# Attention with normalised q and k, then a gated spatial MLP, on one core: the orders of all engines laid out anew, exps that write tokens in natural order, weights and gains loaded otherwise

## The chip, the cores and the metric

One Trainium2 chip, of which the kernel uses one core. A core has a matrix engine (TensorE, PE in the profile; its weight loads are shown apart as PEld), a vector engine (VectorE, DVE), a scalar engine that evaluates functions (ScalarE, ACT), a general engine (GpSimd, POOL) and SyncE (SP), which here issues DMAs only. Operands lie in SBUF, 128 partitions wide; PE writes its results to the eight banks of PSUM, which ACT and DVE read and POOL can't. All engines run at the same time, each through its own queue, in order, and wait for each other by semaphores. The metric is the time of one execution on the device, in microseconds (us).

## What is computed

```python
# q, k, v: (8, 12, 448, 64); all float32
q_n = q / sqrt(mean(q*q, -1) + 1e-6) * g_q
k_n = k / sqrt(mean(k*k, -1) + 1e-6) * g_k
attn = softmax(q_n @ k_n.T / sqrt(64))             # per batch and head, 448 x 448
x = (attn @ v).transpose(0, 2, 1, 3).reshape(8, 448, 768)
h = maximum(x @ w_in, 0)                           # (8, 448, 1024)
u, v = h[..., :512], h[..., 512:]
v_n = (v - mean(v)) / sqrt(var(v) + 1e-6)          # over the 512
v_s = einsum('ts,bsd->btd', w_spatial, v_n) + b_spatial[None, :, None]
out = (u * v_s) @ w_out                            # (8, 448, 768)
```

## The kernel before

The program is a text, `PLAN`: each word names a step, its arguments, the buffers or PSUM banks it takes (after the first slash) and, where there is a choice, the engine (a ACT, v DVE, g POOL, s SP; after the second). The words are carried out from first to last when the program is built, each by the function `op_` of that name, and so the text fixes the order on every engine's queue. There is no scheduler behind it; only the waits are added.

Work is cut into 24 groups of four heads, three to a batch (group G is batch G // 3). A group's q and k come each as a tile of 128 x 2 x 448 numbers: a partition holds seven neighbouring tokens of one head, so that token = 7 p + c, with p the partition's place in its head (64 of them) and c from 0 to 6. The steps of a group:

- `L` (SP) loads raw q (second argument 0) or k (1), 448 KB each. Group 0 comes in four halves of 224 KB, `l.i.r`, and its later steps have small letters for the halves.
- `Q` squares the tile (ACT, POOL or DVE), `R` sums over 64 numbers (DVE), `I` and `J` make 1/rms by a Ln and an Exp (ACT), `N` multiplies and writes bf16 (POOL or DVE).
- `T` turns the tile by a DMA transpose from SBUF to SBUF (SP), and `Z` scales a turned k with the product of the gains (DVE or ACT). In groups 1 to 3 PE turns the tile by seven transposes, `P`, and `K` brings it back from PSUM, scaled if it is a k; for group 0 these are `p` and `k`.
- `S.G.u` makes scores, eight matmuls on parts of the array into two banks, and `E.G.u` takes their exp, 128 x 896 numbers from PSUM to bf16 in SBUF (ACT). There are seven of each per group, 168 in all. The columns of a score bank are q's tokens in the order (c, p).
- `s`, `a`, `b` are passes: they multiply the exps by ones (the softmax's sum) and by the two halves of v. Where the last argument is 1, a step does two groups side by side. `D` and `d` (ACT) make 1/sum, `X` (DVE) scales and writes xt, the turned x.

Then for each batch: `V` and `W` make v's half of x @ w_in, `c` its relu (DVE or ACT), `B`, `M`, `m`, `A` the normalisation, `U` and `u` the other half, `H` the product with the turned w_spatial, `G` the gate, `O` the product with w_out, `o` its copy to SBUF (ACT or DVE), `t` the store. `W.b` also has the last 64 rows of batch b - 1's `O`.

POOL issues the DMAs that cast to bf16: v (`v`), w_in (`wi`), w_spatial (`ws`), w_out (`wo`). `Y` turns w_spatial on PE and `y` copies it to SBUF. Every token axis stays in the order (c, p), so `Y` reads every seventh column of w_sp, the bias is brought into that order by a cast on DVE (`wx`, L337), and `t` writes two DMAs per tile, each of 64 rows that lie seven rows apart in the output. `z.n` issues n dummy matmuls of 128 columns, which compute nothing that is used. `gA`, `gB`, `gC` make a column of g_q * g_k / 8 from two small loads that ACT issues ahead of all else.

DVE and POOL instructions that use both read ports are made to wait for each other, by `port`.

Lines of the profile: L241 and L242 the gains' loads, L260 dummies, L293 and L297 `L` and `l`, L314 `v`, L321 `wi`, L348 `Y`, L361 and L363 copies on ACT and DVE, L367 gA, L380 and L382 squares on ACT and on the others, L393 `R`, L426 `N`, L434 `n`, L445 `P`, L453 `p`, L481 `T`, L506 `S`, L514 `E`, L539 passes, L558 and L562 `D` and `d`, L568 `X`, L575 and L577 relus, L584 `V`, L608 `W`, L645 `U`, L659 `H`, L673 `O`, L690 stores.

Of the kernel before, what the change touches and what calls it, by code (L numbers as in the profile page):

```python
# [25 lines left out]
n.0.1//g p.1.1/0 L.6.1/0 I.2//a S.1.6/67 k.1.1//v S.1.3/12 J.2//a S.1.1/34 L.5.1/1 E.1.6/2/a N.2.0/2/g z.3/f y.0//v  # L26
p.0.1/0 E.1.3/3/a S.1.0/67 k.0.1//v z.10/5 E.1.0/4/a v.0.0//g P.2.0/2 N.2.1/3/v L.6.0/4 z.4/5 E.1.1/5/a wi.1.1//g
s.1.0.0/7 S.1.2/01 Q.3.1/1/v wi.0.2//g P.2.1/6 E.1.2/6/a S.1.4/34 wi.1.0//g z.5/5 K.2.0/2/v E.1.4/7/a Q.4.0/2/g
S.0.3/01 K.2.1/2/v s.1.1.0 s.1.2.0 E.0.3/8/a s.1.3.0 R.3.1//v S.1.5/23 a.1.0.0/6 S.0.6/45 E.1.5/9/a a.1.1.0 Q.4.1/0/g
S.0.5/01 R.4.0//v a.1.2.0 E.0.6/a/a s.1.4.0 s.1.5.0 s.1.6.0 S.2.0/23 E.0.5/b/a b.1.0.0/5 wi.0.0//g Q.3.0/1/v b.1.1.0  # L30
b.1.2.0 b.1.3.0 v.0.3//g E.2.0/c/a S.2.2/01 a.0.0.0/4 a.1.3.0 R.3.0//v Q.5.0/2/g a.1.4.0 D.1/0/a a.1.5.0 a.0.1.0
E.2.2/d/a a.1.6.0 S.0.4/23 R.4.1//v z.4/7 I.3//a S.0.2/01 wi.0.1//g J.3//a E.0.4/e/a b.1.4.0 N.3.0/0/v b.1.5.0
wi.1.2//g b.1.6.0 s.0.0.0/7 E.0.2/f/a s.0.1.0 wi.0.3//g s.0.2.0 N.3.1/1/v S.2.4/23 s.0.3.0 wi.1.3//g z.2/b d.1//a
s.0.4.0 S.2.1/01 I.4//a s.0.5.0 X.1.1//v s.0.6.0 J.4//a z.5/b E.2.1/g/a N.4.1/2/g X.1.0//v P.3.0/5 D.0/1/a P.3.1/6
K.3.0/3/v E.2.4/h/a S.2.3/01 s.2.0.0/7 K.3.1/3/v s.2.1.0 N.4.0/3/g T.4.1/0 b.0.0.0/5 E.2.3/i/a b.0.1.0 R.5.0//v
b.0.2.0 s.2.2.0 b.0.3.0 d.0//a S.3.1/23 b.0.4.0 b.0.5.0 E.3.1/j/a Q.5.1/1/g S.2.5/01 T.4.0/1 b.2.0.0/6 b.2.1.0 b.0.6.0
E.2.5/k/a S.2.6/23 X.0.1//v a.0.2.0 z.2/b L.7.1/5 a.0.3.0 E.2.6/4/a b.2.2.0 Q.6.1/0/g R.5.1//v S.3.3/01 s.2.3.0
s.2.4.0 E.3.3/5/a s.2.5.0 S.3.0/23 a.2.0.0/5 a.2.1.0 I.5//a a.2.2.0 a.2.3.0 R.6.1//v J.5//a s.2.6.0 E.3.0/6/a
N.5.1/0/g a.0.4.0 a.2.4.0 a.0.5.0 a.0.6.0 Q.6.0/2/a b.2.3.0 a.2.5.0 X.0.0//v b.2.4.0 b.2.5.0 D.2/0/a b.2.6.0 R.6.0//v
N.5.0/1/g a.2.6.0 T.5.1/1 S.3.2/01 d.2//a S.3.4/23 U.0.2.0/7 E.3.2/3/a X.2.1//v U.0.2.1 V.0.1.0/4 X.2.0//v v.1.1//g  # L40
# [36 lines left out]
N.13.1/0/g B.2.1//v t.0.3 U.2.2.0/4 E.11.0/2/a V.2.0.2 L.15.0/3 B.2.3//v E.11.2/9/a S.11.6/56 T.13.0/1 S.10.4/23
v.3.4//g U.2.2.1 c.2.0//v E.10.4/4/a U.2.2.2 Z.12/0/v v.3.2//g O.1.0.0/7 T.13.1/1 u.2.2//v E.11.6/k/a N.14.0/3/g
# [82 lines left out]
def kernel(  # L161
# [101 lines left out]
    where = {}  # L263
# [60 lines left out]
    def op_ws(sl, e):  # L324
        pool.dma_start(out=w_sp, in_=moe_w_spatial.rearrange("(p c) s -> p c s", c=C))
# [407 lines left out]
```

## Time and profile before

| | us |
|---|---|
| median of 3 runs (281.03 to 284.57) | 282.72 |
| span of the profiled execution | 277.8 |
| PE busy in it | 261.4 |
| ACT busy | 216.8 |
| DVE busy | 198.7 |
| POOL busy | 155.6 |

The span is the time from the first to the last instruction of one profiled execution; the time of an execution has in addition what lies around that, and the median of the runs is 4.9 us over the span. An instruction group's row gives its line, engine, operation, tiles, shapes and count, then its busy time in us and the mean of one in ns, then the idle time just before its instructions and what ended it. A busy PE is not a PE at its peak: matmuls are pipelined, and the end of one is modelled. The granted clock of TensorE was 0.997 of full speed over the span.

### The profile page before, as it was taken

What the parts mean: (1) busy time and instruction counts of PE and PEld (TensorE: products, weight loads), DVE (VectorE), ACT (ScalarE), POOL (GpSimd) and SP (SyncE); (2) the same over time, 40 slices, a digit from 0 to 9 for tenths busy, and PEclk for the clock granted to TensorE, in tenths of its full rate; (3) what the DMA queues carried; (4) which work ended last, traced back from release to release, by engine and by line L of the source; (5) the groups of instructions that cost most, each with busy time, mean ns of one, the idle gap of its engine ahead of it and who ended that gap; (6) DMA issues with size and microseconds to landing.
All of it is one profiled execution on the core that took longest, in us unless ns stands there. A gap on an engine that the chain in (4) does not pass through costs nothing. (4 is left out here: it accounts for less than half of the span.)

```text
span 277.8 us, 10117 instructions
## 1 busy us (share of the span) xinstructions
PE 261.4 (94%) x4373; PEld 137.4 (49%) x4373; DVE 198.7 (72%) x351; ACT 216.8 (78%) x353; POOL 155.6 (56%) x130
## 2 busy tenths in 40 slices
PE   4799999979999999999999989999998999999993
PEld 4686464435545455354445444453553545455551
DVE  2478978695997997987995677966975174747740
ACT  1399999878999999998999979998898766420632
POOL 3287987987687598957875758645980000000000
PEclk9999999999999999999999999999999999999998
DMA  6989996999989999899999999966589400014586
GB/s 165 331 264 273 176 174 112 217 163 267 257 144 293 311 245 202 179 253 150 257 212 273 228 257 259 181 93 70 75 136 179 161 2 2 18 41 113 138 272 218
DMA packets 62967, 51.14 MB, mean 184 GB/s; under 512 B 39561, under 2 KB 58506, under 8 KB 62922
## 3 DMA queue, kind: packets, MB, share of 16 engines
q1 hardware_dynamic: 54690, 42.22, 64.5%
q0 software_dynamic: 8224, 8.27, 21.2%
q8 instruction: 34, 0.56, 0.8%
q14 instruction: 11, 0.09, 0.1%
q10 hardware_dynamic: 8, 0.00, 0.0%
HBM read 38.55 MB, written 11.01 MB: 178 GB/s over the span
## 5 line engine op out<-in xcount | busy, mean ns | idle before, releaser
L514 ACT ACTIVATE et<-ps 128x896 bf16<-128x896 f32 x168 | 145.7, 921 | 15.0 <-PE ps L506 13.4
L426 POOL TENSOR_TENSOR nrm<-raw,rs 128x896 bf16<-128x896 f32 x43 | 72.2, 1690 | 25.9 <-ACT rs L411 10.1
L506 PE MATMUL ps<-qT,kT 64*32 64x448 bf16 x1344 | 60.2, 354 | 2.5 <-DMA qT<-nrm 1.9
L382 POOL TENSOR_TENSOR sqt<-raw 128x896 f32<-128x896 f32 (+1 forms) x31 | 50.9, 1654 | 17.2 <-DVE vn L636 7.4
L393 DVE TENSOR_REDUCE ss<-sqt 128x14 f32<-128x896 f32 x46 | 48.4, 1075 | 5.0 <-ACT sqt L380 3.8
L539 PE MATMUL ps<-et,vt 64*32 64x448 bf16 x1344 | 48.4, 350 | 2.8 <-DMA vt<-in_v_dram 2.6
L645 PE MATMUL ps<-xt,w_in 128*128 128x448 bf16 x192 | 43.1, 353 | 0.0
L568 DVE TENSOR_TENSOR xt<-ps,rc 128x448 bf16<-128x448 f32 x48 | 28.3, 620 | 14.9 <-ACT rc L562 8.0
L673 PE MATMUL ps<-w_out,gt 128*128 128x384 bf16 x192 | 36.5, 326 | 0.1
L506 PEld LDWEIGHTS <-kT 64*32 64x32 bf16 x1344 | 21.5, 90 | 29.6 <-issue 22.0
L584 PE MATMUL ps<-w_in,xt 128*128 128x512 bf16 x144 | 35.6, 380 | 0.0
L539 PEld LDWEIGHTS <-vt 64*32 64x32 bf16 x1344 | 23.6, 92 | 17.3 <-DMA vt<-in_v_dram 3.9
L664 DVE TENSOR_TENSOR gt<-ps,us 128x448 bf16<-128x448 f32 x32 | 19.3, 620 | 13.0 <-PE ps L659 8.7
L361 ACT ACTIVATE os<-ps 128x384 f32<-128x384 f32 (+1 forms) x33 | 15.9, 493 | 15.4 <-PE ps L673 14.6
L659 PE MATMUL ps<-w_spT,vn 128*128 128x448 bf16 (+1 forms) x128 | 27.7, 353 | 0.0
L645 PEld LDWEIGHTS <-w_in 128*128 128x128 bf16 x192 | 17.0, 98 | 20.5 <-issue 7.3
L539 PE MATMUL ps<-et,ones 64*32 64x448 bf16 x672 | 26.2, 350 | 0.2 <-ACT et L514 0.2
L673 PEld LDWEIGHTS <-gt 128*128 128x128 bf16 x192 | 18.2, 98 | 15.4 <-issue 2.5
L314 POOL DMA_DIRECT2D vt<-in_v_dram x36 | 24.1, 673 | 0.0
L577 DVE TENSOR_SCALAR vs<-ps 128x512 bf16<-128x512 f32 (+1 forms) x24 | 16.3, 684 | 10.4 <-PE ps L584 6.8
L363 DVE COPY os<-ps 128x384 f32<-128x384 f32 (+1 forms) x31 | 16.9, 554 | 8.9 <-PE ps L673 7.7
L620 DVE BATCH_NORM_STATS2 s<-vs 128x6 f32<-128x512 bf16 (+1 forms) x32 | 21.9, 683 | 1.4 <-ACT vs L575 0.9
(62 smaller groups left out, 253.1 us busy)
## 6 DMA issues: line engine op xcount, KB each, us to landing
out_dram<-os SPq DMA_DIRECT2D x56, 192.0 KB, 3.2
raw<-in_q_dram SPq DMA_DIRECT2D x23, 448.0 KB, 5.5
raw<-in_k_dram SPq DMA_DIRECT2D x23, 448.0 KB, 7.0
vt<-in_v_dram POOLq DMA_DIRECT2D x24, 112.0 KB, 5.2
vt<-in_v_dram POOLq DMA_DIRECT2D x12, 224.0 KB, 7.0
w_in<-in_moe_w_in_dram POOLq DMA_DIRECT2D x8, 192.0 KB, 6.1
w_out<-in_moe_w_out_dram POOLq DMA_DIRECT2D x1, 768.0 KB, 11.3
raw<-in_k_dram SPq DMA_DIRECT2D x2, 224.0 KB, 2.6
```

What stands on the lines that cost most here:

```text
L314: pool.dma_start(out=vts[b % 2][64 * halves[0]:64 * halves[0] + 64 * len(halves), g].rearrange("p r c d -> p r (c d)"), in_=src)
L382: port(eng, eng.tensor_tensor(out=t, in0=x, in1=x, op=ALU.mult))
L393: dve.tensor_reduce(out=sss[G % 3][:, i].rearrange("p r c -> p (r c)"), in_=sqt[where.pop(("sq", G, i))].rearrange("p r (c d) -> p (r c) d ...
L426: port(eng, eng.tensor_tensor(out=nrm[sl[0]].rearrange("p c r d -> p r c d"), in0=raw[where["raw", G, i]].rearrange("p r (c d) -> p r c d" ...
L506: pe.matmul(out=ps[at:at + 32, sl[n], 0:S], lhsT=kT[64 * r:64 * r + 64, c, 64 * hh + 32 * x:64 * hh + 32 * x + 32], rhs=qT[64 * r:64 * r + ...
L514: act.activation(out=ets[sl[0]], in_=ps[:, a:b + 1:b - a, 0:S], func=AF.Exp, bias=0.0, scale=1.0)
L539: pe.matmul(out=ps[32 * l:32 * l + 32, where[kind, G][0], 0:S], lhsT=w, rhs=et_of(G, r, c)[at:at + 64], start=(n == 1), stop=(n == C), til ...
L568: dve.tensor_tensor(out=xts[b % 2][:, 2 * g + half, :], in0=ps[:, where.pop(("ab"[half], G))[0], 0:S], in1=rcs[where["rc", G]], op=ALU.mult)
L584: pe.matmul(out=ps[:, bank, :], lhsT=xts[b % 2][:, j, 128 * m:128 * m + 128], rhs=w_in[:, j % 2, j // 2, DH:], start=(n == 1 and j == 2 * ...
L645: pe.matmul(out=ps[:, bank, 0:S], lhsT=w_in[:, j % 2, j // 2, 128 * f:128 * f + 128], rhs=xts[b % 2][:, j, :], start=(n == 1 and j == 2 * ...
L659: pe.matmul(out=ps[:, sl[0], 0:S], lhsT=vns[b % SLOTS["vn"]][rows, m, 128 * f:128 * f + 128], rhs=w_spT[rows, m, :], start=(m == 0), stop= ...
L673: pe.matmul(out=ps[:, sl[0], 0:384], lhsT=gts[b % 2][:, f, 128 * m:128 * m + 128], rhs=w_out[:, f, 384 * h:384 * h + 384], start=(f == 0), ...
```

## The change

All of `PLAN` is rewritten, and some steps with it:

- `E` reads PSUM in the order (p, c), so that exps, and everything behind them, have tokens in their natural order. The inner step of its read is 64 words of four bytes; it writes without gaps, as before.
- w_sp lies as 112 partitions x 4 x 448 and is turned by 16 transposes (49 before), which read it without gaps. The bias is cast by a DMA of POOL straight into w_spT; `wx` is gone.
- `t` stores a tile of 128 rows as one DMA of rows that follow each other, or a half of its columns. There are 34 stores, 56 before.
- w_in comes as six DMAs (eight before), and `V.b.m.g` and `U.b.f.g` need those of their own g alone. The passes g of an accumulation are no longer in the order 0, 1, 2.
- The k gain's load is issued by POOL, ahead of everything else there; g_q stays with ACT.
- 5.1 and 7.0 are turned by PE too (`P` 8 times, 6 before; `T` 38, 40 before).
- Engines, before and after: `Q` ACT 14 and 10, DVE 2 and 6; `N` POOL 43 and 38, DVE 3 and 8; `c` ACT 8 and 17; `K` ACT 1 and 0; the halves' squares `q` DVE 2 and 0, POOL 1 and 3. Between the first and the last exp ACT has 3 `Q` less, 8 `c` and 3 `o` more and a `K` less.
- Dummies: 13 `z` steps with 124 matmuls, then 12 with 183.
- Behind the last `E` there stood 7 `s`, 7 `a`, 7 `b`, 24 `U`, 9 `V`, 21 `O`, 8 `H`, 2 `W`; now 2 `s`, 7 `a`, 2 `b`, 24 `U`, 9 `V`, 22 `O`, 8 `H`, 2 `W`.
- Counted in exps that stand between them, the first step `T` of a group that DMA transposes turn is 4 to 14 ahead of its first `S` before; now 0 to 15, with 3 or less in groups 4, 11, 12, 16, 17 and 21. `N` is 5 or more ahead in both.

The beginning of `PLAN`, and the code:

```diff
-setup//v l.1.0/0 ws//g l.0.0/1 v.0.2//g L.1.0/2 v.0.1//g L.1.1/3 z.30/7 l.0.1 l.1.1 L.2.0/4 L.2.1/5 q.1.0/0/v L.4.1/6
-gA//v gB/7 q.0.0/1/v L.3.1/7 z.33/6 r.0.0//v gC//v r.1.0//v Q.1.0/2/a L.4.0/8 i.0//a R.1.0//v j.0//a n.1.0//g
-Q.1.1/2/a n.0.0//g p.1.0/7 z.7/6 q.0.1//a R.1.1//v q.1.1//g p.0.0/6 k.1.0/0/a Y.1/5 k.0.0/0/v I.1//a Y.3/7 J.1//a
-r.1.1//v y.1//a Y.2/4 N.1.0/0/g Q.2.0/2/a r.0.1//v Y.0/5 y.3//v i.1//a y.2//v Q.2.1/0/a S.0.1/01 R.2.0//v N.1.1/1/g
-S.0.0/23 L.3.0/2 j.1//a P.1.0/7 E.0.1/0/a R.2.1//v z.12/6 K.1.0/1/a n.1.1//g P.1.1/1 L.5.0/3 z.7/6 E.0.0/1/a K.1.1/1/v
...
+setup//v l.0.0/0/s gA//v q.0.0/0/g l.1.0/1/s q.1.0/1/g l.0.1//s q.0.1//g r.1.0//v L.1.0/2/s z.60/f z.2/f gB/0 r.0.0//v
+gC//v r.0.1//v Q.1.0/2/a L.1.1/3/s ws//g l.1.1//s i.0//a L.2.0/4/s v.0.3//g R.1.0//v j.0//a n.1.0//g L.2.1/5/s
+L.3.0/6/s Q.1.1/0/a z.50/f p.1.0/1 q.1.1//a n.0.0//g R.1.1//v I.1//a v.0.0//g v.0.1//g k.1.0/0/v L.3.1/7/s J.1//a
+N.1.0/0/v z.7/f p.0.0/2 k.0.0/0/a z.22/f P.1.0/3 Q.2.0/2/a S.0.2/45 L.4.1/8/s N.1.1/1/g v.0.2//g S.0.0/67 r.1.1//v
+S.0.1/01 i.1//a j.1//a L.5.1/2/s E.0.2/0/a E.0.1/1/a E.0.0/2/a K.1.0/1/v n.0.1//v z.10/f P.1.1/2 z.4/f p.0.1/4
+Q.2.1/0/g K.1.1/1/v z.4/f S.1.1/05 k.0.1//v S.1.3/16 R.2.0//v n.1.1//g R.2.1//v Y.1/7 E.1.1/3/a E.1.3/4/a S.1.2/23
...
-    act.dma_start(out=g_row[:, 1], in_=bass.AP(tensor=g_k.tensor, offset=g_k.offset, ap=[[0, 1], [0, 2], [1, D]]))
+    pool.dma_start(out=g_row[:, 1], in_=bass.AP(tensor=g_k.tensor, offset=g_k.offset, ap=[[0, 1], [0, 2], [1, D]]))
...
-    def op_wi(sl, e, half, l):
-        x = bass.AP(tensor=moe_w_in.tensor, offset=moe_w_in.offset + (64 * l + 32 * half) * DF,
-                    ap=[[DF, 32], [256 * DF, NG], [1, DF]])
-        pool.dma_start(out=w_in[32 * l:32 * l + 32, half, :, :], in_=x)
+    def op_wi(sl, e, g, half):
+        x = bass.AP(tensor=moe_w_in.tensor, offset=moe_w_in.offset + (256 * g + 32 * half) * DF,
+                    ap=[[64 * DF, 4], [DF, 32], [1, DF]])
+        pool.dma_start(out=w_in[:, half, g, :], in_=x)
...
-        pool.dma_start(out=w_sp, in_=moe_w_spatial.rearrange("(p c) s -> p c s", c=C))
+        pool.dma_start(out=w_sp, in_=moe_w_spatial.rearrange("(c p) s -> p c s", p=RW))
...
-        sync.dma_start(out=oss[-1][64:65, 0:S], in_=moe_b_spatial.rearrange("(o s) -> o s", o=1))
+        pool.dma_start(out=w_spT[64:65, 3, :], in_=moe_b_spatial.rearrange("(o s) -> o s", o=1))
...
-        for a in range(n):
-            for c in range(C):
-                pe.matmul(out=p_[64 * a:64 * a + 64, T * c:T * c + T],
-                          lhsT=w_sp[:, c, :].rearrange("q (p c) -> q c p", c=C)[:, 2 * m + a, :],
-                          rhs=ident[0:64, 0:64], is_transpose=True, start=(c == 0), stop=(c == C - 1),
-                          tile_position=(0, 64 * a))
+        for c in range(S // RW):
+            pe.matmul(out=p_[0:n, RW * c:RW * c + RW], lhsT=w_sp[:, c, 128 * m:128 * m + n], rhs=ident[0:RW, 0:RW],
+                      is_transpose=True, start=(c == 0), stop=(c == S // RW - 1))
...
-        act.activation(out=ets[sl[0]], in_=ps[:, a:b + 1:b - a, 0:S], func=AF.Exp, bias=0.0, scale=1.0)
+        act.activation(out=ets[sl[0]].rearrange("q n (p c) -> q n p c", c=C),
+                       in_=ps[:, a:b + 1:b - a, 0:S].rearrange("q n (c p) -> q n p c", c=C),
+                       func=AF.Exp, bias=0.0, scale=1.0)
...
-        for par in ((0, 1) if m < 3 else (1,)):
-            engines[(e or "ss")[par]].dma_start(out=out_c[b][2 * m + par if m < 3 else 6], in_=t[64 * par:64 * par + 64])
+        rows = slice(0, 128) if m < 3 else slice(64, 128)
+        cols = slice(0, DM) if h is None else slice(384 * h, 384 * h + 384)
+        assert all(where["o", b, m, n] for n in ((0, 1) if h is None else (h,)))
+        engines[e or "s"].dma_start(out=out[b, 128 * m:128 * m + rows.stop - rows.start, cols], in_=t[rows, cols])
```

More of the change, by code (lines that the diff above doesn't have):

```diff
@@ L26 @@
[L26 to L40, printed above, removed]
@@ L182 @@
     TAIL = 384
+    RW = 112
     scale = 1.0 / math.sqrt(D)
@@ L223 @@
     w_out = const.tile([128, 4, DM], BF, name="w_out")
-    w_sp = const.tile([64, C, S], BF, name="w_sp")
+    w_sp = const.tile([RW, S // RW, S], BF, name="w_sp")
     w_spT = const.tile([128, 4, S], BF, name="w_spT")
@@ L316, in op_v @@
         where.setdefault(("v", b, g), set()).update(halves)
[L318 to L322 removed]
+    def op_wi(sl, e, g, half):
+        x = bass.AP(tensor=moe_w_in.tensor, offset=moe_w_in.offset + (256 * g + 32 * half) * DF,
+                    ap=[[64 * DF, 4], [DF, 32], [1, DF]])
+        pool.dma_start(out=w_in[:, half, g, :], in_=x)
+        where["wi", g, half] = True
     def op_ws(sl, e):
[L325 removed]
+        pool.dma_start(out=w_sp, in_=moe_w_spatial.rearrange("(c p) s -> p c s", p=RW))
     def op_wo(sl, e):
@@ L582, in op_V @@
         for j in (2 * g, 2 * g + 1):
-            assert where["x", b, j] and all(where["wi", h, l] for h in range(2) for l in range(4))
+            assert where["x", b, j] and where["wi", g, 0] and where["wi", g, 1]
             pe.matmul(out=ps[:, bank, :], lhsT=xts[b % 2][:, j, 128 * m:128 * m + 128], rhs=w_in[:, j % 2, j // 2, DH:],
@@ L643, in op_U @@
         for j in (2 * g, 2 * g + 1):
-            assert where["x", b, j] and all(where["wi", h, l] for h in range(2) for l in range(4))
+            assert where["x", b, j] and where["wi", g, 0] and where["wi", g, 1]
             pe.matmul(out=ps[:, bank, 0:S], lhsT=w_in[:, j % 2, j // 2, 128 * f:128 * f + 128], rhs=xts[b % 2][:, j, :],
@@ L654, in op_H @@
         where["H", b, f] = sl[0]
-        assert where["wx"]
+        assert where["wb"]
         for m in range(4):
@@ L682, in op_o, with op_t @@
         where["o", b, m, h] = True
-    out_c = [out[b].rearrange("(p c) m -> c p m", c=C) for b in range(B)]
-    def op_t(sl, e, b, m):
+    def op_t(sl, e, b, m, h=None):
         t = oss[where["os", b, m]]
-        assert where["o", b, m, 0] and where["o", b, m, 1]
-        for par in ((0, 1) if m < 3 else (1,)):
-            engines[(e or "ss")[par]].dma_start(out=out_c[b][2 * m + par if m < 3 else 6], in_=t[64 * par:64 * par + 64])
+        rows = slice(0, 128) if m < 3 else slice(64, 128)
+        cols = slice(0, DM) if h is None else slice(384 * h, 384 * h + 384)
+        assert all(where["o", b, m, n] for n in ((0, 1) if h is None else (h,)))
+        engines[e or "s"].dma_start(out=out[b, 128 * m:128 * m + rows.stop - rows.start, cols], in_=t[rows, cols])
     def op_z(sl, e, n):
```

257 lines of the change are left out of this document (134 added, 123 removed).

## The prediction

> **What bounds the kernel now.** I read the page's first lines, then busy time by stage (columns: busy us of PE, PEld, DVE, ACT, POOL; granted clock; DMA share; GB/s).
>
> ```profile
> span 277.8 us, 10117 instructions
> L514 ACT ACTIVATE et<-ps 128x896 bf16<-128x896 f32 x168 | 145.7, 921 | 15.0 <-PE ps L506 13.4 <-PE ps L539 0.8
> ```
> ```profile
> 0.00:18.56 18.56, 13.09 (x151) 11.94 (x151) 9.21 (x22) 8.02 (x14) 8.18 (x14) 1.00 0.88 258
> 18.56:60.00 41.44, 39.45 (x737) 21.25 (x729) 33.27 (x46) 39.16 (x59) 35.87 (x33) 1.00 1.01 189
> 60.00:233.37 173.37, 169.03 (x3145) 82.91 (x3146) 132.68 (x238) 155.44 (x248) 111.60 (x85) 1.00 0.94 190
> 233.37:272.90 39.53, 39.53 (x364) 21.29 (x348) 23.49 (x48) 13.52 (x31) 0.00 (x0) 1.00 0.42 118
> 272.90:277.80 4.90, 0.29 (x2) 0.00 (x0) 0.00 (x0) 0.65 (x2) 0.00 (x0) 0.80 0.58 189
> ```
>
> Four stages. A ramp of 18.56 us in which no exp runs. A middle of 214.8 us from the first exp to the end of the last, where ACT is busy 39.16 + 155.44 = 194.6 us and PE 208.5. There ACT sets the pace at first (39.16 of 41.44); later both are nearly full, and ACT's waits, 13.4 us in all, are for score matmuls. A tail of 39.5 us with PE busy to the last tenth. Then 4.9 us for the last copies and stores. So a gain must come from an earlier first exp, from fewer waits in the middle, or from less PE work left for the tail.
>
> **The ramp.** The timeline of the ramp (start, duration, instruction, what the idle before it waited for):
>
> ```profile
> 1.69 3.38 PE L260 MATMUL ps<-ident 128*128 128x128 bf16 x30 [1.69 <-POOL ident masks.py:199]
> ...
> 1.97 0.58 ACTq L242 DMA_DIRECT2D g_row<-in_g_k_dram  x1
> ...
> 8.18 0.28 DVE L367 SCALAR_TENSOR_TENSOR g_row<-g_row 1x128 f32<-1x128 f32 x1 [4.18 <-DMA g_row<-in_g_k_dram]
> ...
> 9.02 3.70 PE L260 MATMUL ps<-ident 128*128 128x128 bf16 x33
> ...
> 10.60 0.95 ACT L380 ACTIVATE sqt<-raw 128x896 f32<-128x896 f32 x1 [6.73 <-DMA raw<-in_q_dram]
> ...
> 11.78 0.21 ACT L419 ACTIVATE rs<-ls 128x14 f32<-128x14 f32 x1
> ...
> 12.07 1.84 POOL L434 TENSOR_TENSOR nrm<-raw,rs 128x448 bf16<-128x448 f32 x2 [8.46 <-ACT rs L419]
> ...
> 14.58 3.42 PE L348 MATMUL ps<-ident,w_sp 64*64 64x64 bf16 x49
> ...
> 17.94 0.94 PE L506 MATMUL ps<-qT,kT 64*32 64x448 bf16 x16
> ...
> 18.56 0.92 ACT L514 ACTIVATE et<-ps 128x896 bf16<-128x896 f32 x1 [0.17 <-PE ps L506]
> ...
> 19.21 0.83 PE L260 MATMUL ps<-ident 128*128 128x128 bf16 x12
> ...
> 19.41 0.92 ACT L361 ACTIVATE qT<-ps 128x896 bf16<-128x896 bf16 x1
> ...
> 21.73 1.73 ACT L514 ACTIVATE et<-ps 128x896 bf16<-128x896 f32 x2
> ```
> ```profile
> raw<-in_q_dram SPq DMA_DIRECT2D x1, 224.0 KB, 2.7
> raw<-in_q_dram SPq DMA_DIRECT2D x1, 448.0 KB, 8.9
> ```
> ```profile
> 0.00:5.00 5.00, 3.31 (x30) 3.12 (x30) 1.84 (x9) 1.28 (x1) 2.57 (x9) 1.00 0.58 154
> 5.00:10.00 5.00, 1.56 (x13) 1.48 (x13) 1.79 (x5) 0.00 (x0) 0.00 (x0) 1.00 1.04 245
> ```
>
> Before, three things hold the first exp back. DVE stands on gA for 4.18 us, for a gain row that lands 6.2 us after its issue. ACT's first square waits to 10.60 for a 448 KB load (8.9 us), with w_sp and v loads beside it. And 49 transposes of w_sp, 3.42 us, stand on PE ahead of the first score.
>
> The change takes each away. The k gains are POOL's first DMA; three of the four first half squares move to POOL, ahead of its w_sp and v loads, so no square stands behind gA on DVE any more (the two reductions still do, and gC, which waits for gB behind 62 dummies on PE, holds the reductions of group 1 to about 8, when they aren't due yet); the 16 transposes left of w_sp go behind the first scores, where dummies fill PE anyway, so they cost nothing there (as long as exps set the pace). Worked along: half loads land at 3.4 to 3.9 (2.7 us after issue); POOL's squares, at
>
> ```profile
> L426 POOL TENSOR_TENSOR nrm<-raw,rs 128x896 bf16<-128x896 f32 x43 | 72.2, 1690 | 25.9 <-ACT rs L411 10.1 <-DVE us L577 5.0 <-issue 4.9
> ...
> L393 DVE TENSOR_REDUCE ss<-sqt 128x14 f32<-128x896 f32 x46 | 48.4, 1075 | 5.0 <-ACT sqt L380 3.8 <-POOL sqt L382 0.9
> ...
> L426 DVE TENSOR_TENSOR nrm<-raw,rs 128x896 bf16<-128x896 f32 x3 | 3.2, 1090 | 0.4 <-ACT rs L411 0.4
> ...
> L382 POOL TENSOR_TENSOR sqt<-raw 128x448 f32<-128x448 f32 x1 | 0.9, 931 | 0.0
> ```
>
> 0.93 each, end near 6.2, and only then come w_sp and v.0.3. If the k gains still take 6.2 us they land near 7, and the reductions of half 0 (half of 1075 ns each) end near 8.2, no later than Q.1.0 below. By 5 us 770 KB have come at 154 GB/s, then 245 KB a us: the three half loads and L.1.0 (1120 KB) are in by about 7, L.1.1 (1568 KB) by about 9.3 with w_sp beside it. Q.1.0 0.95, Ln and Exp 0.5 give rs of the first half near 8.9; before it was 11.99. From there two halves on POOL (1.84), transpose and eviction need 3.7: k.0.0 is done near 12.6. But S.0.2 stands behind P.1.0 on PE, and that behind N.1.0 on DVE: L.1.1 9.3, square to 10.3, reduction 11.3, Ln and Exp 11.9, N.1.0 13.0, transposes 13.5; S.0.2 takes 0.6 to its exp, as before (17.94 to 18.56). First exp near 14.0: **-4.5 us**. Lower bound -5.5 (L.1.1 a us earlier). Upper bound 0: the 112 dummies ahead of p.1.0 at 0.112 each (3.38/30, 3.70/33) end near 15, and the first exp comes near 18.5. I take a first third at that pace and the rest at 0.07 (0.83/12, the row that began right behind other work): done by 11, in time.
>
> The Trainium skill, TensorE: Matmul & The Clock Gate, Part 1, says the array runs at half clock until some 3.4 us of sustained work; the granted clock reads 1.00 throughout and cannot show it, but the three dummy rows agree, and by it the dummies end in time.
>
> Then before, ACT copied a qT (0.92) and waited between its first exps: four took from 18.56 to 23.46. The changed order puts three behind each other and that copy on DVE; **-1.0** (bounds -1.5 and 0, if K.1.1 is late).
>
> **The middle.** ACT also gives three squares away (-3 x 0.945) and takes eight relus and three output copies:
>
> ```profile
> L380 ACT ACTIVATE sqt<-raw 128x896 f32<-128x896 f32 x14 | 13.2, 945 | 7.6 <-DMA raw<-in_q_dram 6.7 <-DVE ss L393 0.7
> L361 ACT ACTIVATE os<-ps 128x384 f32<-128x384 f32 x27 | 13.2, 496 | 14.9 <-PE ps L673 14.6
> ...
> L575 ACT ACTIVATE vs<-ps 128x512 bf16<-128x512 f32 x6 | 3.5, 597 | 0.9 <-PE ps L584 0.9
> ...
> L445 PE MATMUL ps<-ident,nrm 128*128 128x128 bf16 x42 | 3.3, 219 | 0.0
> ```
>
> 8 x 0.60 + 3 x 0.50 - 2.8 = +3.5 us, of which the 13.4 us of waits swallow over half: **+1.5** (0 to 3.5). DVE, 33.27 of 41.44 early and 132.68 of 173.37 later, has room for five more norms and four more squares. Two more tiles turned by PE cost 2 x 0.55 (3.3 us for six) and save two DMA transposes: nothing on balance. Each norm or square moved from POOL to DVE saves POOL 1.69 and costs DVE 1.09 on the port that the two take in turns, and POOL has idle time to give: 0. w_in in six loads by group: its consumers come after group 0's exps, so 0, unless the loads on POOL delay N.2 or N.3, +1 at most. The bias goes straight into w_spT, and a cast leaves DVE: 0, DVE had room. The stores, half as many and the same bytes, stand on SP between the same loads: 0.
>
> The chain that ended last has one wait late in the middle, and then PE without a gap:
>
> ```profile
> 205.95 1.79 SPq L481
> 207.85 7.97 DMA qT<-nrm
> 215.95 0.38 PE ps L506 x8
> ...
> 232.99 3.53 PE ps L539 x144
> ...
> 237.78 0.65 PE ps L673 x4
> ```
> ```profile
> ACT et L514 <- PE ps L506: 13.4, 30, 2.0
> ```
>
> Three norms in a row on POOL sent the last transposes late, and the scores and exps behind them waited; the exp at 216.4 is ACT's longest wait for a score in the row of all such waits (13.4 us in 30 times, the longest 2.0). In the changed order N.22 and N.23 stand 10 to 17 exps ahead of their scores (8 to 10 before) and one is on DVE: **-1.5** (0 to -2.0); next late would be T.23.0, four exps ahead.
>
> **The tail** keeps the same work but for passes: 11 double passes are left behind the last exp instead of 21, at 3.53/18 = 0.196 each, -2.0; one more O, +0.65: **-1.3**. What leaves the tail enters a middle where PE is nearly full: **+0.7** (half; 0 to 1.3). The stores' end: 0.
>
> Sum: -4.5 - 1.0 + 1.5 - 1.5 - 1.3 + 0.7 = -6.1, a span of 271.7. The median of the runs, 282.7, is 4.9 over the profiled span; with that, **276.6 us**.
>
> **The rivals.**
>
> (1) The exps slow down. They now read PSUM with 256 bytes from element to element. No row has such a read. Bounds:
>
> ```profile
> L382 DVE TENSOR_TENSOR sqt<-raw 128x448 f32<-128x448 f32 x2 | 1.2, 615 | 1.1 <-DMA raw<-in_k_dram 1.1
> ...
> L337 DVE CAST w_spT<-os 1x448 bf16<-1x448 f32 x1 | 1.0, 968 | 0.0
> ```
>
> The cast read every seventh word: 968 ns where a plain pass over 448 took 615, 1.57 times. At that, an exp takes 1450 ns and 168 of them add 89 us: 366 us. Below nothing isn't possible: the elements are as many. I take 0, by the nearest rows, ACT reading PSUM: 896 elements cost it 0.92 us at 2 bytes an element (the qT copy at 19.41) and 0.921 at 4 (the exps), so its pace there goes by the element and not by the bytes or lines that it touches; the cast was DVE on SBUF. The rival wins from 6.1/168 = 36 ns an exp; from 70 ns the kernel is over 2% slower.
>
> The Trainium skill speaks for this rival: PSUM — Partial Sum Buffer, Specifications, gives PSUM lines of 8 bytes and says a non-contiguous pattern slows matmuls much. That is said of PE's access; no run here shows ACT's, and by it alone the time would lie near this rival's.
>
> (2) PE sets the pace from about 40 us on, the early exps only wait longer later, or the dummies end late: 281 to 283.
>
> (3) Transposes come late: some groups' DMA transposes now stand 3 exps or less ahead of their scores instead of 4 and more. Three waits such as the 2.0 us one and slower recovery would cost the ramp's gain and more: 285 to 290. Against it: SP issues them as soon as the norm is there, and norms stand 5 exps ahead at least in both.
>
> (4) The middle's other waits fall too: 10 of the 13.4 us go, 268 to 271.
>
> **How the numbers follow.** 2% of 282.7 is 5.7 us, about what a measurement of this kernel can tell from no change; faster means under 277.1. The forecast has 0.62 and by its bounds 271 to 283: 0.40 under 277.1, 0.22 within. Rival 1 has 0.20 (0.04 within 2%, 0.16 slower), since nothing in the trace excludes it; rival 2 0.08 (within 0.07, slower 0.01); rival 3 0.06 (0.01, 0.05); rival 4 0.04. Faster 0.44, same 0.34, slower 0.22. The range of 269 to 290 leaves out rival 1 where it costs over 80 ns an exp and half of rival 4.
>
> **What would show it.** First exp near 14 and gA before 5; the exps' mean at 921; no wait of PE for a DMA transpose over 1 us; PE without a gap behind the last exp for about 38 us. An exp mean over 957, or a first exp after 17, would make it wrong.

## The result, and the profile after

| | before | after |
|---|---|---|
| median of the runs, us | 283.64 (281.03 to 285.06, 4 runs) | 375.47 (371.61 to 378.30, 4 runs) |
| ratio of the times, with its 95% interval | | 1.318 (1.303 to 1.333) |
| time of the profiled execution, us | | 377.19 |
| its span, us | 277.8 | 375.4 |
| ACT busy in it, us | 216.8 | 223.0 |
| PE busy in it, us | 261.4 | 288.2 |

The changed kernel is slower by almost a third. The prediction, 276.6 us with a range of 269 to 290, was wrong. The ratio is taken from the two faster of the changed kernel's four executions (spans of 369.8 and 372.0 us), while the profiled one is of the two slower ones, so a difference taken from its span of 375.4 may be 3 to 6 us too large.

Busy time by stage of the changed kernel, cut as before at the first exp, at 60 us, and at the end of the last exp (columns as in the prediction):

```profile
0.00:14.45 14.45, 9.44 (x180) 8.45 (x184) 8.44 (x19) 6.85 (x12) 9.90 (x17) 1.00 0.89 270
14.45:60.00 45.55, 32.68 (x507) 16.01 (x500) 19.63 (x27) 23.13 (x33) 20.81 (x18) 0.63 0.55 116
60.00:333.22 273.22, 208.31 (x3477) 94.07 (x3483) 153.70 (x264) 180.06 (x283) 118.57 (x93) 0.96 0.61 132
333.22:375.40 42.18, 37.76 (x266) 20.52 (x252) 22.29 (x45) 13.02 (x29) 0.00 (x0) 1.00 0.36 132
```

The ramp is 4.1 us shorter (14.45 for 18.56), the end behind the last exp 2.2 us shorter (42.18 for 44.4). The middle has grown from 214.8 to 318.8 us. No engine is full there any more: from 14.45 to 60 ACT is busy for 23.13 of 45.55 us and PE for 32.68, and the granted clock falls to 0.63.

The costliest groups (busy us and mean ns of one, then the idle time just before and what ended it):

```profile
L509 ACT ACTIVATE et<-ps 128x896 bf16<-128x896 f32 x168 | 149.4, 916 | 105.0 <-PE ps L501 32.7 <-PE ps L536 32.3 <-PE ps L581 8.6
L501 PE MATMUL ps<-qT,kT 64*32 64x448 bf16 x1344 | 71.1, 379 | 27.0 <-ACT et L509 26.1 <-DVE vs L574 0.2
L536 PE MATMUL ps<-et,vt 64*32 64x448 bf16 x1344 | 57.0, 376 | 15.5 <-ACT et L509 15.4
L642 PE MATMUL ps<-xt,w_in 128*128 128x448 bf16 x192 | 45.6, 357 | 10.9 <-ACT et L509 10.8
L565 DVE TENSOR_TENSOR xt<-ps,rc 128x448 bf16<-128x448 f32 x48 | 28.2, 620 | 46.6 <-ACT rc L559 17.6 <-ACT et L509 15.9 <-PE ps L536 9.2
```

An exp with its new read takes 916 ns, no more than before (921). What has grown is the idle time ahead of it, from 15.0 to 105.0 us, and much of it ended with work that has nothing to do with scores: 32.3 us with passes (L536), 8.6 with `V` (L581). It goes both ways. `U` (L642) waited 10.8 us for exps, though it reads xt and w_in and writes a bank of its own; `X` on DVE (L565) waited 15.9 us for exps. Before, the exps waited 0.8 us for passes, and neither `U` (L645 there) nor `X` (L568) for an exp:

```profile
L645 PE MATMUL ps<-xt,w_in 128*128 128x448 bf16 x192 | 43.1, 353 | 0.0
L568 DVE TENSOR_TENSOR xt<-ps,rc 128x448 bf16<-128x448 f32 x48 | 28.3, 620 | 14.9 <-ACT rc L562 8.0 <-PE ps L539 6.9
```

One place shows what they are. The timeline of the changed kernel near 62 us (start, duration, instruction, idle time before it):

```profile
61.06 0.39 PE L501 MATMUL ps<-qT,kT 64*32 64x448 bf16 x8
61.20 1.16 DVE L565 TENSOR_TENSOR xt<-ps,rc 128x448 bf16<-128x448 f32 x2 [1.01 <-PE ps L536]
...
62.23 0.92 ACT L509 ACTIVATE et<-ps 128x896 bf16<-128x896 f32 x1 [0.58 <-DVE xt L565]
...
63.19 0.62 DVE L565 TENSOR_TENSOR xt<-ps,rc 128x448 bf16<-128x448 f32 x1 [0.83 <-ACT et L509]
63.20 1.30 PE L642 MATMUL ps<-xt,w_in 128*128 128x448 bf16 x6 [1.76 <-ACT et L509]
...
64.86 0.57 PE L501 MATMUL ps<-qT,kT 64*32 64x448 bf16 x16
65.31 2.54 ACT L509 ACTIVATE et<-ps 128x896 bf16<-128x896 f32 x3 [1.32 <-PE ps L501]
```

By `PLAN`, the exp at 62.23 is `E.3.3`, whose scores lie in banks 2 and 6. They are there by 61.45. Yet the exp waits for an `X` on DVE, which reads group 1's result in bank 4 (`X.1.0`, the first of the two at 61.20; it ends at 61.84); and once it runs, `U.0.2.0`, which writes bank 3, stands on PE until it is over, and `X.2.1`, which reads bank 5, stands on DVE. The next scores, `S.3.1`, stand behind `U` in PE's queue and start at 64.86, so the next exp is late as well. (They take bank 2, which this exp does read, so before its end at 63.15 they could not have started in any case.) Banks 3, 4 and 5 are neither read nor written by this exp. They lie between the two that it reads.

That is the part of the change that neither the list of it nor the prediction names. In the old `PLAN` the two banks of an `S` are always neighbours. In the new one they are in 43 of 168; the others lie 2 to 7 apart (`S.3.3/26`), with 1.9 banks between on average over all. Theory N: the program is put in order, when it is built, as if an exp used everything from its first bank to its last. Two other theories are tried beside it: R, that the new read with its steps of 256 bytes holds PSUM up for PE and DVE, and O, that the new orders of the engines are too tight by themselves.

### The profile page after: what moved, and what is told of

Read it like the earlier page. It is cut to its first block, busy times and chain, and to the rows that moved or that the text cites. A ratio compares the mean times of both kernels' runs of the same rounds, so it can differ in the third digit from the quotient of the medians.

```text
span 375.4 us, 10169 instructions
## 1 busy us (share of the span) xinstructions
PE 288.2 (77%) x4398; PEld 139.1 (37%) x4413; DVE 204.1 (54%) x353; ACT 223.0 (59%) x355; POOL 149.3 (40%) x126
## 4 chain that ended last, share of the span: by engine, by line
PE 58%; ACT 29%; DVE 5%; issue 4%; DMA 2%; SPq 0%; another core or an unknown queue 0%; ACTq 0%; DVEq 0%
ACT et L509 26%; PE ps L536 14%; PE ps L501 10%; PE ps L670 9%; PE ps L642 8%; PE ps L581 6%; PE ps L656 5%; PE ps L605 3%; DMA raw<-in_k_dram 2%; DVE xt L565 1%; DVE ss L388 1%; PE ps L440 1%; ACT rc L555 1%; DVE gt L661 1%; PE ps L264 1%
## 5 line engine op out<-in xcount | busy, mean ns | idle before, releaser
L509 ACT ACTIVATE et<-ps 128x896 bf16<-128x896 f32 x168 | 149.4, 916 | 105.0 <-PE ps L501 32.7
L421 POOL TENSOR_TENSOR nrm<-raw,rs 128x896 bf16<-128x896 f32 x38 | 63.9, 1687 | 75.8 <-ACT rs L406 27.6
L501 PE MATMUL ps<-qT,kT 64*32 64x448 bf16 x1344 | 71.1, 379 | 27.0 <-ACT et L509 26.1
L377 POOL TENSOR_TENSOR sqt<-raw 128x896 f32<-128x896 f32 (+1 forms) x33 | 53.0, 1610 | 59.1 <-DVE vn L633 17.5
L536 PE MATMUL ps<-et,vt 64*32 64x448 bf16 x1344 | 57.0, 376 | 15.5 <-ACT et L509 15.4
L642 PE MATMUL ps<-xt,w_in 128*128 128x448 bf16 x192 | 45.6, 357 | 10.9 <-ACT et L509 10.8
L565 DVE TENSOR_TENSOR xt<-ps,rc 128x448 bf16<-128x448 f32 x48 | 28.2, 620 | 46.6 <-ACT rc L559 17.6
L536 PE MATMUL ps<-et,ones 64*32 64x448 bf16 x672 | 37.5, 385 | 9.3 <-ACT et L509 9.3
L581 PE MATMUL ps<-w_in,xt 128*128 128x512 bf16 x129 | 35.8, 379 | 8.1 <-ACT et L509 6.7
L536 PEld LDWEIGHTS <-vt 64*32 64x32 bf16 x1344 | 25.6, 97 | 35.3 <-issue 27.6
L656 PE MATMUL ps<-w_spT,vn 128*128 128x448 bf16 (+1 forms) x128 | 29.5, 369 | 1.9 <-ACT et L509 1.9
L642 PEld LDWEIGHTS <-w_in 128*128 128x128 bf16 x192 | 17.8, 98 | 32.0 <-issue 18.7
L574 DVE TENSOR_SCALAR us<-ps 128x448 bf16<-128x448 f32 x24 | 14.8, 624 | 26.9 <-PE ps L642 18.0
```

The lines of the kernel that those rows point to most:

```text
L377: port(eng, eng.tensor_tensor(out=t, in0=x, in1=x, op=ALU.mult))
L421: port(eng, eng.tensor_tensor(out=nrm[sl[0]].rearrange("p c r d -> p r c d"), in0=raw[where["raw", G, i]].rearrange("p r (c d) -> p r c d" ...
L501: pe.matmul(out=ps[at:at + 32, sl[n], 0:S], lhsT=kT[64 * r:64 * r + 64, c, 64 * hh + 32 * x:64 * hh + 32 * x + 32], rhs=qT[64 * r:64 * r + ...
L509: act.activation(out=ets[sl[0]].rearrange("q n (p c) -> q n p c", c=C), in_=ps[:, a:b + 1:b - a, 0:S].rearrange("q n (c p) -> q n p c", c= ...
L536: pe.matmul(out=ps[32 * l:32 * l + 32, where[kind, G][0], 0:S], lhsT=w, rhs=et_of(G, r, c)[at:at + 64], start=(n == 1), stop=(n == C), til ...
L565: dve.tensor_tensor(out=xts[b % 2][:, 2 * g + half, :], in0=ps[:, where.pop(("ab"[half], G))[0], 0:S], in1=rcs[where["rc", G]], op=ALU.mult)
```

## The experiments

All ratios are against the kernel before, run in the same batch, with 95% intervals. Where none is given, the kernel ran once, for its profile.

**e1: neighbouring pairs, nothing else.** All words and their order are those of the changed kernel; only bank numbers differ. A score bank is taken again a median of 8 words of `PLAN` after its exp in both.

```diff
-N.1.0/0/v z.7/f p.0.0/2 k.0.0/0/a z.22/f P.1.0/3 Q.2.0/2/a S.0.2/45 L.4.1/8/s N.1.1/1/g v.0.2//g S.0.0/67 r.1.1//v
+N.1.0/0/v z.7/f p.0.0/2 k.0.0/0/a z.22/f P.1.0/7 Q.2.0/2/a S.0.2/56 L.4.1/8/s N.1.1/1/g v.0.2//g S.0.0/34 r.1.1//v
...
-Q.2.1/0/g K.1.1/1/v z.4/f S.1.1/05 k.0.1//v S.1.3/16 R.2.0//v n.1.1//g R.2.1//v Y.1/7 E.1.1/3/a E.1.3/4/a S.1.2/23
+Q.2.1/0/g K.1.1/1/v z.4/f S.1.1/45 k.0.1//v S.1.3/01 R.2.0//v n.1.1//g R.2.1//v Y.1/7 E.1.1/3/a E.1.3/4/a S.1.2/23
```

> The changed kernel with its order of work word for word, but every pair of score banks put next to each other (in the changed kernel 125 of the 168 pairs are not neighbours, in the kernel before none). Theory N (an exp over two banks is ordered against all work in the banks that lie between them): the loss goes, 270 to 281 us, exp 0.92 us each, ACT idle ahead of the exps under 25 us instead of 105. Theory R (the read with 256-byte steps holds PSUM up for PE and DVE): it stays, 360 to 380 us. Theory O (the new orders of the engines are too tight by themselves): it stays over 340 us.

Measured: 273.06 us (271.02 to 273.54), ratio 0.966 (0.958 to 0.974), span 271.8. The exps' row and the stages, first exp at 15.47 and last one's end at 229.49:

```profile
L509 ACT ACTIVATE et<-ps 128x896 bf16<-128x896 f32 x168 | 145.6, 919 | 12.9 <-PE ps L501 12.1
```
```profile
0.00:15.47 15.47, 10.85 (x180) 9.70 (x184) 8.60 (x20) 6.66 (x13) 10.63 (x18) 0.89 0.91 273
15.47:60.00 44.53, 41.21 (x808) 20.36 (x800) 35.49 (x52) 41.17 (x65) 37.25 (x31) 1.00 1.03 203
60.00:229.49 169.49, 166.50 (x3181) 82.31 (x3182) 134.87 (x238) 154.74 (x251) 101.41 (x79) 1.00 0.96 188
229.49:271.80 42.31, 37.96 (x272) 20.36 (x251) 22.29 (x45) 13.03 (x30) 0.00 (x0) 0.99 0.36 131
```

The whole loss is gone, and the order of the work was not its cause: theory O falls. The place shown above, in this version:

```profile
39.69 1.89 DVE L565 TENSOR_TENSOR xt<-ps,rc 128x448 bf16<-128x448 f32 x3 [1.38 <-PE ps L536]
...
39.91 1.31 PE L642 MATMUL ps<-xt,w_in 128*128 128x448 bf16 x6
...
40.38 0.92 ACT L509 ACTIVATE et<-ps 128x896 bf16<-128x896 f32 x1
...
42.34 1.73 ACT L509 ACTIVATE et<-ps 128x896 bf16<-128x896 f32 x2 [0.19 <-PE ps L501]
```

`X` three times, `U` six times and the exp run beside each other, and the next exps follow 1.96 us after it (3.08 in the changed kernel).

**e2: the kernel before, with the strided exps alone.**

```diff
-        act.activation(out=ets[sl[0]], in_=ps[:, a:b + 1:b - a, 0:S], func=AF.Exp, bias=0.0, scale=1.0)
+        act.activation(out=ets[sl[0]].rearrange("q n (p c) -> q n p c", c=C),
+                       in_=ps[:, a:b + 1:b - a, 0:S].rearrange("q n (c p) -> q n p c", c=C),
+                       func=AF.Exp, bias=0.0, scale=1.0)
```

> The kernel before with its own order and its neighbouring pairs, and only the exps' access changed to that of the changed kernel (the rows of the output then come in another order). N: no change, 281 to 286 us, exp 0.92 us. R: 340 to 380 us. O: no change, 281 to 286 us.

Measured: 288.56 us (279.89, 286.54, 290.58 and 294.13), ratio 1.022 (1.002 to 1.042); the kernel before took 281.06 to 298.02 in that batch. The median lies over the 286 of the forecast, but the spread is that of the kernel before, and the profiled execution, 279.89 us with a span of 278.1, is below all eight of its executions. A loss is not shown.

```profile
L514 ACT ACTIVATE et<-ps 128x896 bf16<-128x896 f32 x168 | 145.6, 921 | 16.1 <-PE ps L506 14.3
```

The exp's duration is that of before to the nanosecond, and its idle time 16.1 for 15.0. Theory R, which had 340 us or more, falls. The spread leaves room for some per cent, which e9 looks at.

**e3: the kernel before, with its banks renamed** so that all pairs lie 3 or 5 apart; order and exps unchanged.

```diff
-S.0.0/23 L.3.0/2 j.1//a P.1.0/7 E.0.1/0/a
+S.0.0/16 L.3.0/2 j.1//a P.1.0/5 E.0.1/0/a
```

> The kernel before, order and exps unchanged, with only the bank numbers renamed (bank x becomes 3x modulo 8), so that all 168 pairs lie 3 or 5 banks apart. N: 330 to 420 us, with waits of exps for passes and of passes for exps that the kernel before doesn't have. R and O: no change, 281 to 286 us.

Measured: 405.12 us, span 403.4.

```profile
L514 ACT ACTIVATE et<-ps 128x896 bf16<-128x896 f32 x168 | 151.4, 916 | 123.6 <-PE ps L506 39.9 <-PE ps L539 27.2 <-PE ps L584 11.2
```

Names of banks alone, with nothing else of the change, make a loss of this kind, and a larger one, and the same waits (exps for passes 27.2 us, for `V` 11.2) appear in a kernel that did not have them (0.8 us for passes before). The renaming leaves the number of words until a bank is taken again as it was. The trace also records waits as instructions of their own: the exps' line has 30 EVENT_SEMAPHORE instructions in the kernel before and 67 in e3. So the program itself, and not only its pace, waits for more.

**e4: the changed kernel with plain exps**, its far pairs kept (the edit of e2 the other way round).

> The changed kernel, its order and its banks as they are, with the exps reading and writing in plain order as in the kernel before (the token order of the output then differs from the stores). N: no gain, 365 to 380 us. R: 270 to 281 us. O: no gain, 365 to 380 us.

Measured: 379.4 us, exp 916 ns, 105.3 us of idle time ahead of the exps: no gain. With e1 to e4 both factors have been tried on both kernels, and only the banks matter.

**e5: one exp for each bank.** Is it the range, or do banks far apart cost something in the chip?

```diff
-        act.activation(out=ets[sl[0]].rearrange("q n (p c) -> q n p c", c=C),
-                       in_=ps[:, a:b + 1:b - a, 0:S].rearrange("q n (c p) -> q n p c", c=C),
-                       func=AF.Exp, bias=0.0, scale=1.0)
+        for n, x in enumerate((a, b)):
+            act.activation(out=ets[sl[0]][:, n].rearrange("q (p c) -> q p c", c=C),
+                           in_=ps[:, x, 0:S].rearrange("q (c p) -> q p c", c=C),
+                           func=AF.Exp, bias=0.0, scale=1.0)
```

> The changed kernel, its order and its far pairs as they are, but each exp as two instructions of 448 elements, one for each bank, so that no exp's range goes over another bank. Theory N (the order put on the range between the banks): from the rows of 448 and 512 elements each half takes about 0.55 us, 0.18 us more per pair, 30 us of ACT in all, of which the 13 us of ACT's waits in the neighbouring version swallow some: 285 to 305 us, with ACT's idle ahead of the exps under 40 us. Rival D (banks that lie far apart cost time in the chip itself, whatever the order): 375 us and more.

Measured: 280.10 us, span 278.3, under the forecast's lower end.

```profile
L510 ACT ACTIVATE et<-ps 128x448 bf16<-128x448 f32 x336 | 156.5, 572 | 12.8 <-PE ps L501 12.3
```

Banks, order and amount of work are those of the changed kernel, and the false waits are gone. So banks far apart cost nothing here by themselves; it takes one instruction over two of them. That the order comes from the program as it is built, and not from the chip, rests on the waits themselves, which the profile reads from semaphore events, and on the added wait instructions of e3. The code that puts the program in order was not looked at. The price of the split was put too high (below).

**e7: all pairs with exactly one bank between.** Bank numbers alone, again.

> The changed kernel, its order as it is, each of the 168 pairs exactly two apart, with one bank between (in the changed kernel 1.9 banks between on average, in the neighbouring version none). N: between the two, by the count of banks between some 325 us (300 to 350). A theory by which only the order of work matters has it at 273 or at 375.

Measured: 352.97 us, span 351.2.

```profile
L509 ACT ACTIVATE et<-ps 128x896 bf16<-128x896 f32 x168 | 148.4, 917 | 82.8 <-PE ps L501 29.9 <-PE ps L536 21.5 <-PE ps L581 9.5
```

In the span none between costs 0, one between 79 us, 1.9 on average 104 us (351.2 and 375.4 less 271.8). Theory N's direction held. Its forecast by simple proportion, 325, was 28 us low, and its range ended at 350: the cost is not in proportion to the count of banks between.

**e8: neighbours in another choice of banks.**

> The changed kernel's order with neighbouring pairs, in another choice of banks (each freed bank left alone longer before it is taken again). If the waits of exps for scores that are left (12 us) come from banks taken again too early: 268 to 272 us; if they come from PE being full: 271 to 275 us, as the first choice.

Measured: 273.20 us (270.10 to 275.43), ratio 0.953 (0.943 to 0.964), not told apart from e1; exps waited 14.2 us for scores (12.1 in e1). Neither of the two choices of banks tried takes these last waits away.

**e9: e1 with plain exps.**

> The neighbouring version with plain exps as in the kernel before (the rows of the output then come in another order): what the 256-byte steps of the exps' reads cost where nothing else is in the way. The prediction's term: nothing, 270 to 275 us and 0.92 us an exp. If the steps cost something that the waits of the changed kernel hid: over 5 us faster than the neighbouring version, under 267 us.

Measured: 271.87 us (270.02 to 278.42), ratio 0.956 (0.941 to 0.971), exp 918 ns. Against e1's ratio, 0.966 (0.958 to 0.974), that is no difference that can be told. The two intervals leave room for a cost of the 256-byte steps of up to some 3%; the duration of an exp (918 ns, 919 in e1) shows none.

The last three take the ramp apart, on the version with neighbouring pairs. **e6: the k gains back on ACT's queue.**

```diff
-    pool.dma_start(out=g_row[:, 1], in_=bass.AP(tensor=g_k.tensor, offset=g_k.offset, ap=[[0, 1], [0, 2], [1, D]]))
+    act.dma_start(out=g_row[:, 1], in_=bass.AP(tensor=g_k.tensor, offset=g_k.offset, ap=[[0, 1], [0, 2], [1, D]]))
```

> The version with neighbouring pairs, but the k gains loaded behind the q gains on ACT's queue again. If the ramp's gain hangs on this load as the prediction has it (the reductions of the first half stand on DVE behind gA), first exp 1 to 3 us later than in the neighbouring version (15.5 us) and 1 to 3 us more in all, 274 to 277 us; if the gain row lands in time on either queue: no change.

Measured: 272.11 us (270.11 to 273.20), ratio 0.956 (0.949 to 0.964): no change.

**e10 and e11: the loads of w_sp and of a v part in front again**, with the k gains on POOL and on ACT.

```diff
-setup//v l.0.0/0/s gA//v q.0.0/0/g l.1.0/1/s
+setup//v l.0.0/0/s ws//g v.0.3//g gA//v q.0.0/0/g l.1.0/1/s
```

> The neighbouring version with the loads of w_sp and of one v part put back in front of the first squares on POOL, the k gains still POOL's first load. The gain row landed in time on either queue in the run before this one, so what held it back in the kernel before (gA at 8.18 us) should be the bulk loads issued beside it: if bulk loads alone do it, gA after 6 us here, first exp after 17 us and 274 to 278 us. If the gain row is safe in front of them on POOL: gA before 5 us, first exp before 16.5 us, 270 to 274 us.

> Both at once: w_sp and v in front, and the k gains on ACT's queue behind the q gains, as the kernel before has them. Gain row late by both causes together: gA at 7 to 9 us, first exp 17 to 19 us, 274 to 278 us. If gA stays before 6 us, neither the queue nor these loads made the ramp's gain, and the squares moved off DVE did.

Measured: 276.39 us (274.77 to 278.02), ratio 0.974 (0.963 to 0.985), and 278.90 us (276.60 to 280.88), ratio 0.980 (0.964 to 0.996). From the timelines of e6, e10 and e11: gA, the squares of the first two whole tiles, the first exp.

```profile
5.03 0.30 DVE L362 SCALAR_TENSOR_TENSOR g_row<-g_row 1x128 f32<-1x128 f32 x1 [2.80 <-DMA g_row<-in_g_k_dram]
...
7.97 0.95 ACT L375 ACTIVATE sqt<-raw 128x896 f32<-128x896 f32 x1 [4.12 <-DMA raw<-in_q_dram]
...
9.28 1.40 ACT L375 ACTIVATE sqt<-raw 128x896 f32<-128x896 f32 x2
...
15.20 2.54 ACT L509 ACTIVATE et<-ps 128x896 bf16<-128x896 f32 x3 [0.21 <-PE ps L501]
```
```profile
4.13 1.85 DVE L362 SCALAR_TENSOR_TENSOR g_row<-g_row 1x128 f32<-1x128 f32 x1 [1.91 <-DMA g_row<-in_g_k_dram]
...
9.38 0.95 ACT L375 ACTIVATE sqt<-raw 128x896 f32<-128x896 f32 x1 [6.14 <-DMA raw<-in_q_dram]
...
11.87 0.95 ACT L375 ACTIVATE sqt<-raw 128x896 f32<-128x896 f32 x1 [1.10 <-DMA raw<-in_k_dram]
...
17.65 0.92 ACT L509 ACTIVATE et<-ps 128x896 bf16<-128x896 f32 x1 [0.69 <-PE ps L501]
```
```profile
5.71 0.28 DVE L362 SCALAR_TENSOR_TENSOR g_row<-g_row 1x128 f32<-1x128 f32 x1 [3.48 <-DMA g_row<-in_g_k_dram]
...
10.22 0.95 ACT L375 ACTIVATE sqt<-raw 128x896 f32<-128x896 f32 x1 [6.35 <-DMA raw<-in_q_dram]
...
13.11 1.42 ACT L375 ACTIVATE sqt<-raw 128x896 f32<-128x896 f32 x2 [1.50 <-DMA raw<-in_k_dram]
...
18.90 0.92 ACT L509 ACTIVATE et<-ps 128x896 bf16<-128x896 f32 x1 [0.80 <-PE ps L501]
```

Both expectations tied the first exp to gA, and e10 fits neither of its two cases: gA is early (4.13) and the first exp late all the same (17.65, with 15.47 in e1). In e11 gA stays before 6 us (5.71), by which its expectation would credit the squares moved off DVE. But they are off DVE in e11 too, and the first exp comes at 18.90. What moved is two loads of 448 KB. ACT's first square waits for `L.1.0` and starts at 8.0 to 8.4 us with w_sp behind (e6, e1), at 9.4 and 10.2 with w_sp in front. The next one, of `L.1.1`, moves further: 9.3 and 9.7 us (e6, e1), then 11.9 and 13.1. The first exp starts 5.7 to 5.9 us after this second square in all four. So in these runs, with one profile each, the ramp's gain goes with the order of the bulk loads: 2.2 us of it are lost in e10 and all of it in e11 (18.90, for 15.47 in e1 and 18.56 before). The gain row costs nothing on either queue by itself (e6).

The Trainium skill (Trainium Kernel Development and Optimization, Key Constraints) says that DMAs issued by SP, ACT and POOL run on the same DMA engines and interleave. These runs agree: with POOL's w_sp and v in front, the square that waits for SP's `L.1.0` starts 1 to 2 us later.

The best version is the changed kernel with neighbouring pairs: e1, 3.4% faster than the kernel before (2.6 to 4.2). e6 and e8 read 4.4 and 4.7%, and the three are not told apart.

## Why the prediction was wrong

**The step that failed** is the sum of the middle, +1.5, -1.5 and +0.7, in which the new bank numbers stand for nothing. The rival on the exps asked for the exp's price and said "I take 0, by the nearest rows". It weighed how long the instruction takes, and there 0 was right (916 to 921 ns in every kernel with whole exps). Nowhere did the prediction ask what the instruction is ordered against. `PLAN` shows the pairs, `S.0.0/23` before and `S.1.1/05`, `S.1.3/16` after in the quoted diff, and the prediction counted steps, engines and exps between steps without looking at banks. What the runs show in its place: exps over banks that aren't neighbours wait for the work in the banks between and hold it up (e1, e3, e5), and the term that was missing is +105 us (318.8 less 214.0 in e1).

**Rival 1** had the size nearly right, 366 us, but by luck, since its mechanism was wrong: no exp became slower. Its test, "an exp mean over 957", would have passed the kernel, and so would the other, a first exp after 17. Neither test looked at idle time. The Trainium skill's rule that it named (PSUM — Partial Sum Buffer, Specifications: a non-contiguous pattern slows matmuls) does not carry over to ACT's reads here, by 921 ns in e2.

**The other terms** can be read from e1, where the missing one is zero. Its span is 271.8 us and the prediction's was 271.7, by terms that err both ways, so that the close match is partly luck:

- Ramp, -4.5: -3.1 in e1 (15.47) and -4.1 in the changed kernel (14.45, forecast 14.0). With the same order the first exp came between 13.9 (e7) and 15.7 us (e9), 5.0 to 5.8 us behind the square of `L.1.1`, the load with which the prediction's own chain ends. The prediction named three things that hold the ramp up. The loads, with w_sp and v beside them, are shown to be one of them (e10, e11); the k gains' queue alone isn't (e6); no run put the 49 transposes back.
- First exps, -1.0: the first four took 3.95 us (15.47 to 19.42) in e1, 4.90 before: -0.95.
- ACT's middle, the late stall and the passes, +1.5 - 1.5 + 0.7: with the -1.0, -0.3 forecast for the whole middle, and -0.8 measured (214.0 for 214.8). They were not told apart; the exps' waits for scores fell from 13.4 to 12.1 us. ACT's busy time there rose by 1.3 us (195.9 for 194.6), not by the 3.5 counted.
- Tail, -1.3: -2.1 from the last exp to the end (42.3 for 44.4).
- From span to time, +4.9: the profiled executions of e1 and of the changed kernel took 1.7 and 1.8 us more than their spans (273.54 and 377.19). The 4.9 compared a span with the median of other executions, and most of it was the difference between executions. With 1.7 the sum would have been 273.4, for 273.06 measured in e1.

**The dummies** ended in time, as forecast, but were misread. The prediction took the 112 ahead of `p.1.0` at 128 columns each and had them done by 11. All dummies of the changed kernel have `/f`, for which the code takes 64 columns (`ident[:, 0:128 if bank < 8 else 64]`), so the 128 columns said of `z` above hold for the numbers below 8 alone. They were done by 8.7 us:

```profile
2.60 3.49 PE L264 MATMUL ps<-ident 128*128 128x64 bf16 x62 [2.60 <-POOL ident masks.py:199]
...
6.54 2.17 PE L264 MATMUL ps<-ident 128*128 128x64 bf16 x50
```

**Rivals 2 to 4** did not decide: e1's middle is no longer than before, no matmul of e1 waits for a DMA transpose (rival 3), and 12.1 of the 13.4 us of waits are left (rival 4). In the changed kernel their prices are lost in the 104 us.

## What to carry to other kernels

When buffers are renamed or laid out anew, look at every instruction whose access jumps over some of them. It may be ordered against all work on what lies between, and an edit that leaves every duration as it was can cost a third of the time. A wait between two steps that share no data, in a row that the kernel before did not have, is the sign; neighbours, or an instruction for each part, are the cure. And an instruction's price is its duration and its order: a test of a forecast that looks only at durations can't fail for the second reason.

## What the hardware showed that was not expected

- ACT reads PSUM in steps of 256 bytes at its full pace: 896 elements in 916 to 921 ns, as without steps.
- Two exps of 448 elements behind each other cost little more than one of 896. Each is shown with 572 ns, but they overlap: 156.5 us busy for 168 pairs is 0.93 us a pair, against 0.87 (145.6 / 168) for one instruction. The estimate had 0.18 us more a pair; it is 0.065.
- From 14.45 to 60 us of the changed kernel the granted TensorE clock was 0.63, with PE busy for 72% of the time; in e1 it was 1.00 with 93% (41.21 of 44.53). Matmuls of passes took 376 ns over the run, 350 in e1. The Trainium skill (TensorE: Matmul & The Clock Gate, Part 1) has the clock gated by how busy PE is, and the rows agree for this stretch. How many of the 104 us the clock took, beside the waits that made PE idle, was not measured. It can't be most of them: when `E.3.3` starts, the changed kernel is 23 us behind e1, both counted from the first exp (62.23 less 14.45, and 40.38 less 15.47), and the rest is lost behind 60 us, where the granted clock was 0.96.
